# Queries as rows of eight tokens, weights in 512 KB pieces, output rows in threes, mp by head pairs

## The chip, the cores and the metric

The kernel runs on one core of a Trainium2 chip. The metric is the device time of one execution in microseconds. Its parts are named by their engines: PE is TensorE (PEld its weight loads), DVE is VectorE, ACT is ScalarE, POOL is GpSimd, SP is SyncE, whose queue issues all DMAs of this kernel.

## What is computed

Attention through 32 packed queries per head, and then a soft mixture of experts over all tokens, all in float32:

```
batch, n_heads, seq, head_dim = 8, 8, 576, 64;  n_pack = 32      # q, k, v: [8, 8, 576, 64], p: [8, 8, 32, 64]
N, D, E, S_per_e, F = 4608, 512, 8, 4, 1024                      # phi: [512, 32], w1: [8, 512, 1024], w2: [8, 1024, 512]

p_packed = sm_attn(p, k, v)                 # softmax(p k^T / 8) v
out      = sm_attn(q, p_packed, p_packed)   # softmax(q p_packed^T / 8) p_packed
x = out.transpose(0, 2, 1, 3).reshape(4608, 512)

logits = x @ phi                            # [4608, 32]
d = softmax of logits over the tokens;  slot_input = d.T @ x
h = relu(slot_input[e] @ w1[e]);  slot_out[e] = h @ w2[e]        # 4 slots for each of 8 experts
c = softmax of logits over the slots
return c @ slot_out                         # [4608, 512]
```

## The kernel before

The batches go in four pairs (`dd`) and the heads in two groups of four (`g`), so that there are eight steps `i = 2 dd + g`, each with both batches of its pair (`b2`). A step loads k, q and v tiles (lines 105 to 142), each in a main tile of 1 MB from a pool `ring` of 15 buffers and a small tail tile of 128 KB; the tails of v and q share six buffers (`NTAIL`). All loads are issued by SP in program order. A main tile of v and of q holds for each of 128 partitions four tokens of a head side by side (runs of 1 KB); the tail holds the last 64 tokens of a head in 64 partitions per batch.

For each step, `kp` transposes k, `s1` makes the first scores and their exponentials, `ap` and `at` transpose those, `ppm` multiplies with v, `ppn` and `pt` (lines 302 to 328) normalise the packed rows and transpose them into `ppT`, in which the two halves of the partitions (the first token's 64 columns and the second's) stand in two separate slots `x`, the rest being zero. `mp` (line 330) multiplies `ppT` with `phi`, head by head. `qp` (line 348) transposes q in 18 blocks of 128 columns, two tokens in each, and `s2p` (line 367) multiplies them with `ppT` in three chunks `c` (two with four rows of tokens, one with the ninth). `a2p` and `lg` give the logits, and the functions `f1` to `gsa` carry the softmax over the tokens from one pair to the next. The steps are interleaved by hand in the loop from line 752 on: the loads of step i + 1 stand at its head, the loop works step i, and the last step and what follows stand in an order written out by hand.

The weights come in 32 chunks of 1 MB (`load_w`, line 720), each in four DMAs of 256 KB with runs of 2 KB. They go to `ring` buffers as these come free, and to buffers of pools that close. The first three are issued in the last turn of the loop, between the main tiles and the tails of v and q of step 7 (lines 761 to 765). Layer 1 (`layer1a`, line 977) and layer 2 (`layer2`, line 1032) take the chunks in order; the last expert's second layer (`last2`, line 1116) is split in column halves and ends the work on weights.

After the softmax over the slots, `cq` and `cp` (lines 1050 to 1072) split and transpose its result into `cT`, nine blocks of 128 tokens for each pair, and `slot_out` (line 1147) multiplies each block with the slots' rows into a 256 KB tile of the output. Eight of the nine blocks of a pair go out by batch, four rows per partition (runs of 8 KB, DMAs of 1 MB; the first four tiles singly, the first of them in two halves); the ninth blocks of all pairs are collected in `ot` and stored at the end by two DMAs of 512 KB, 64 partitions each, in runs of 2 KB. `evac` (line 81) shares the copies out of PSUM among ScalarE and VectorE.

Of the kernel before, what the change touches and what calls it, by code (L numbers as in the profile page):

```python
# [23 lines left out]
def pack_attention_soft_moe(  # L24
# [90 lines left out]
    def load_rows(src, i, name):  # L115

        dd, g = divmod(i, NG)
        main = ring.tile([P, 2, 4, TB * D], F32, tag="ring", name=f"{name}_{i}")
        for b2 in range(2):
            xs = src[2 * dd + b2, 4 * g : 4 * g + 4]  # L120
# [4 lines left out]
        return main  # L125

    def load_tail(src, i, name):
        dd, g = divmod(i, NG)
        tail = vpool.tile([P, 4, D], F32, tag="tail", bufs=NTAIL, name=f"{name}x_{i}")
        for b2 in range(2):  # L130
            xs = src[2 * dd + b2, 4 * g : 4 * g + 4]
# [4 lines left out]
        return tail  # L136

    def load_q(i):
        qts[i] = load_rows(q, i, "q"), load_tail(q, i, "q")

    def load_v(i):
        vts[i] = load_rows(v, i, "v"), load_tail(v, i, "v")
# [175 lines left out]
    def pt(i):  # L318

        s = st[i]  # L320
        tp = s["m"][:, P : 3 * P]
        for b2 in range(2):
            nc.tensor.transpose(
                tp[:, b2 * P : (b2 + 1) * P], s["ppd"][:, b2].rearrange("p x d -> p (x d)"), ident
            )
        tpv = tp.rearrange("p (b h s) -> p b h s", b=2, h=4)
        nc.vector.tensor_copy(ppT[0:D, :, :, 0, :], tpv[0:D])
        nc.vector.tensor_copy(ppT[D:P, :, :, 1, :], tpv[D:P])

    def mp(i):  # L330

        g = i % NG
        s = st[i]
        mq = s["m"][:, 3 * P : 3 * P + 2 * NSLOT]
        for b2 in range(2):
            for h in range(4):
                nc.tensor.matmul(
                    mq[32 * h : 32 * h + 32, b2 * NSLOT : (b2 + 1) * NSLOT],
                    ppT[:, b2, h, h % 2, :],
                    phi_sb[:, 2 * g + h // 2, :],  # L340
                    start=True,
                    stop=True,
                )
        mm = lpool.tile([P, 2, NSLOT], F32, tag="mm", bufs=2, name=f"mm_{i}")
        nc.scalar.copy(mm.rearrange("p b x -> p (b x)"), mq)
        s["mm"] = mm

    def qp(i, m0, eng=None):

        s = st[i]  # L350
        main, tail = qts[i]
        if m0 == 0:
            s["qT"] = tpool.tile([P, 2 * T, P], F32, tag="qT", name=f"qT_{i}")
        qf = (main if m0 < 16 else tail).rearrange(
            "p b h x -> p (b h x)" if m0 < 16 else "p h x -> p (h x)"
        )
# [10 lines left out]
    def s2p(i, c):  # L367
# [384 lines left out]
    for i in range(NSTEP - 1):  # L752
# [297 lines left out]
    def cq(t0, nt=4):  # L1050
# [10 lines left out]
        for x in range(0, nt, 4):  # L1061
            c4s[t0 + x] = c4[:, x : x + 4]

    def cp(t0, eng="act"):
        tp = bank(pstr, f"cp_{t0}")
        for j in range(4):
            nc.tensor.transpose(
                tp[:, j * P : (j + 1) * P].bitcast(F32R),
                c4s[t0][:, j].rearrange("p a b s -> p (a b s)"),
                identr,  # L1070
            )
        evac(cT[:, t0 : t0 + 4].rearrange("p t x -> p (t x)"), tp, eng)

    with tc.manual_schedule(engines={EP.PE, EP.DVE, EP.Activation, EP.Pool}):
# [14 lines left out]
        for t0 in (0, 4):  # L1089
            cp(t0)  # L1090
# [54 lines left out]
    ot = ring.tile([P, ND, DM], F32, tag="ring", name="ot")  # L1145
# [6 lines left out]
    todo = list(range(8, NT, 4))  # L1152
    for dd in range(ND):
        for b2 in range(2):
            ob = ring.tile([P, TB, DM], F32, tag="ring", name=f"ob_{dd}_{b2}")
            r0 = (2 * dd + b2) * S
            ov = out[r0 : r0 + TB * P].rearrange("(p t) m -> p t m", t=TB)
            for t in range(TB):
                o = 4 * (t % 2) + 2 * b2 + t // 2
                if (dd, b2, t) == (0, 0, 0):  # L1160

                    for xs, eng in zip(halves, ("act", "dve")):
                        op = bank(pstr, f"op_0_0_0_{eng}")
                        nc.tensor.matmul(op[:, xs], cT[:, o, :], sh[:, xs], start=True, stop=True)
                        evac(ob[:, t, xs], op[:, xs], eng)
                        nc.sync.dma_start(out=ov[:, t, xs], in_=ob[:, t, xs])
                    continue
                slot_out(ob[:, t], f"{dd}_{b2}_{t}", dd * T + o)
                n = 1 if (dd, b2) == (0, 0) else TB
                if (t + 1) % n == 0:  # L1170
                    ts = slice(t + 1 - n, t + 1)
                    nc.sync.dma_start(out=ov[:, ts], in_=ob[:, ts])
            for x in range(2 if dd == 0 else 1):
                if todo:
                    cp(todo.pop(0), None)
        slot_out(ot[:, dd], f"{dd}", dd * T + T - 1)
    for b2 in range(2):
        nc.sync.dma_start(
            out=out.rearrange("(a b s) m -> b s a m", b=2, s=S)[b2, TB * P : S],
            in_=ot[b2 * R : (b2 + 1) * R],  # L1180
        )
# [32 lines left out]
```

## Time and profile before

| what | value |
|---|---|
| median of three runs | 227.0 us (225.78, 227.0, 228.66) |
| the profiled execution, whole time | 227.74 us |
| its span, first to last instruction | 225.9 us |
| its mean granted TensorE clock | 0.953 |
| busy, share of the span | PE 85%, DVE 53%, ACT 51%, POOL 11% |
| moved by DMA | 72.36 MB, mean 320 GB/s |

A share of busy time is a mean over stages that have different limits, so it is read together with the slices, the chain of waits and the single stretches. Times inside the profile count from the start of the span. The terms of the working below are in the profiled execution's own time, which is 0.7 us above the median.

### The profile page before, as it was taken

The page shows a single profiled execution, that of the slowest core. Times are in us where ns is not written, and L with a number is a line of the kernel's source. Part 1 is how long each engine was busy: PE and PEld are TensorE (multiplying, and loading weights), DVE is VectorE, ACT ScalarE, POOL GpSimd, SP SyncE. Part 2 cuts the span into 40 slices and gives each one's busy share as a digit, 9 for nine tenths or more (in the row PEclk, how much of TensorE's full clock was granted, in tenths as well). Part 3 has the DMA queues.
Part 4 walks back from the last instruction along what each step waited for, and adds up shares of the span by engine and source line. Part 5 has one row for each costly group of instructions (what it writes and reads, how often), then busy time and mean ns, then how long its engine had stood idle before and what let it go on. Part 6 is the DMA issues. An engine that isn't in the chain of part 4 may idle for free.

```text
span 225.9 us, 6900 instructions
## 1 busy us (share of the span) xinstructions
PE 191.9 (85%) x2875; PEld 129.6 (57%) x2875; DVE 120.3 (53%) x279; ACT 115.9 (51%) x253; POOL 25.1 (11%) x40
## 2 busy tenths in 40 slices
PE   1897799898996999999999989988899999899500
PEld 1665577585683678668678758766534333465200
DVE  2220576257287146728956626896777260388500
ACT  2377536956843475684675694755322100288500
POOL 3000003103003000300210120042030000000000
PEclk9999979999998599999999999999999999999955
DMA  4999999999999999999799999999999999089996
GB/s 134 299 273 311 323 304 315 282 285 317 284 320 272 335 291 331 314 366 326 218 328 382 377 389 380 364 369 357 384 354 376 385 392 375 25 281 418 424 395 159
DMA packets 52624, 72.36 MB, mean 320 GB/s; under 512 B 12656, under 2 KB 32368, under 8 KB 51696
## 3 DMA queue, kind: packets, MB, share of 16 engines
q1 hardware_dynamic: 52592, 71.91, 98.6%
q8 instruction: 23, 0.38, 0.7%
q14 instruction: 9, 0.07, 0.1%
HBM read 62.46 MB, written 9.44 MB: 318 GB/s over the span
## 4 chain that ended last, share of the span: by engine, by line
PE 63%; ACT 16%; DVE 6%; DMA 4%; issue 3%; SPq 1%; ACTq 0%; DVEq 0%
PE s L380 9%; PE kp L220 8%; PE s L240 7%; PE hp L987 6%; PE so L1036 5%; ACT a L251 5%; PE m L294 4%; PE op L1149 3%; PE qp L361 3%; PE gr L634 3%; ACT kT L88 3%; DMA k<-in_k_dram 2%; ACT qT L88 2%; PE a2p L452 2%; PE ap L269 2%
## 5 line engine op out<-in xcount | busy, mean ns | idle before, releaser
L88 ACT COPY kT<-kp 128x512 f32<-128x512 f32 (+1 forms) x42 | 19.1, 483 | 25.3 <-PE kp L220 25.3
L443 POOL TENSOR_TENSOR a<-a,z 128x1152 f32<-128x1152 f32 (+1 forms) x8 | 16.0, 1995 | 72.5 <-DVE z L442 50.1
L380 PE MATMUL s<-ppT,qT 128*64 128x64 f32 x576 | 21.3, 231 | 1.4 <-ACT qT L88 0.9
L220 PE MATMUL kp<-ident,k 128*128 128x128 f32 x128 | 20.9, 307 | 1.9 <-DMA k<-in_k_dram 0.9
L88 ACT COPY qT<-qp 128x512 f32<-128x512 f32 (+1 forms) x40 | 20.3, 559 | 4.1 <-PE qp L361 3.8
L380 PEld LDWEIGHTS s<-ppT,qT 128*64 128x64 f32 x576 | 19.1, 144 | 4.9 <-ACT qT L88 3.5
L251 ACT ACTIVATE a<-s,nm 128x576 f32<-128x576 f32 x16 | 21.6, 1350 | 0.5 <-DVE nm L247 0.5
L247 DVE TENSOR_REDUCE nm<-s 128x1 f32<-128x576 f32 x16 | 11.9, 746 | 18.0 <-PE s L240 18.0
L240 PE MATMUL s<-kT,pT 64*32 64x288 f32 x256 | 17.4, 446 | 3.8 <-ACT kT L88 3.2
L220 PEld LDWEIGHTS kp<-ident,k 128*128 128x128 f32 x128 | 16.1, 157 | 7.3 <-issue 2.3
L390 DVE TENSOR_REDUCE mx<-s 128x16 f32<-128x512 f32 (+1 forms) x24 | 12.6, 551 | 12.5 <-PE s L380 12.4
L361 PE MATMUL qp<-ident,q 128*128 128x128 f32 x128 | 18.4, 281 | 0.0
L88 ACT COPY a1T<-ap 128x512 f32<-128x512 f32 x16 | 8.7, 588 | 18.8 <-PE ap L269 18.8
L361 PEld LDWEIGHTS qp<-ident,q 128*128 128x128 f32 x128 | 15.4, 146 | 1.9 <-issue 1.9
L987 PE MATMUL hp<-w,xz 128*32 128x512 f32 x128 | 14.8, 594 | 0.5 <-DVE xz L1075 0.5
L435 DVE TENSOR_REDUCE z<-a 128x36 f32<-128x1152 f32 (+2 forms) x9 | 10.9, 1207 | 6.2 <-ACT a L426 6.2
L1036 PE MATMUL so<-w,hT 128*32 128x512 f32 x112 | 12.4, 592 | 0.0
L1149 PE MATMUL op<-sh,cT 128*128 128x512 f32 x35 | 11.9, 444 | 0.2 <-ACT ob L88 0.2
L452 PE MATMUL a2p<-ident,a 128*128 128x128 f32 x72 | 11.0, 280 | 0.6 <-ACT a L412 0.6
L88 ACT COPY ob<-op 128x512 f32<-128x512 f32 x19 | 10.7, 588 | 1.6 <-PE op L1149 0.5
L88 ACT COPY a2T<-a2p 128x512 f32<-128x512 f32 (+1 forms) x24 | 11.1, 514 | 0.6 <-PE a2p L452 0.5
L396 DVE TENSOR_TENSOR a<-s,mx 128x512 f32<-128x512 f32 (+1 forms) x21 | 10.9, 549 | 0.1
(155 smaller groups left out, 302.0 us busy)
## 6 DMA issues: line engine op xcount, KB each, us to landing
w<-in_moe_w_dram SPq DMA_DIRECT2D x128, 256.0 KB, 5.4
k<-in_k_dram SPq DMA_DIRECT2D x16, 512.0 KB, 6.6
q<-in_q_dram SPq DMA_DIRECT2D x16, 512.0 KB, 7.3
v<-in_v_dram SPq DMA_DIRECT2D x16, 512.0 KB, 8.1
out_dram<-ob SPq DMA_DIRECT2D x7, 1024.0 KB, 6.6
kx<-in_k_dram SPq DMA_DIRECT2D x16, 64.0 KB, 6.3
qx<-in_q_dram SPq DMA_DIRECT2D x16, 64.0 KB, 7.1
vx<-in_v_dram SPq DMA_DIRECT2D x16, 64.0 KB, 6.7
```

The costliest lines, as they stand in the source:

```text
L88: nc.scalar.copy(dst, src)
L220: nc.tensor.transpose(tp[:, j * P : (j + 1) * P], src, ident)
L240: nc.tensor.matmul(ps[hs, x, 0:HALF], pTs[dd][xs, g, 4 * b2 + h].rearrange("p a s -> p (a s)"), kT[xs, :, hs], start=True, stop=True,)
L251: nc.scalar.activation(a1.rearrange("p (r t x) -> p x t r", t=T, x=2), ps[:, :, 0:HALF].rearrange("p x (t r) -> p x t r", t=T), AF.Exp, bi ...
L361: nc.tensor.transpose(tp[:, j * P : (j + 1) * P], qf[:, o : o + P], ident)
L380: nc.tensor.matmul(ps[us, j * 64 : j * 64 + 64], s["qT"][:, 8 * c + j, us], w, start=True, stop=True)
L390: nc.vector.tensor_reduce(mx, s[f"s2{c}"], axis=AX.X, op=ALU.max)
L443: eng.tensor_tensor(a2, a2, z2.unsqueeze(3).broadcast_to([P, nt, 4, NS]), op=ALU.mult)
L452: nc.tensor.transpose(tp[:, j * P : (j + 1) * P], s["a2"][:, t0 + j].rearrange("p h s -> p (h s)"), ident)
L987: nc.tensor.matmul(hp[nh][32 * a : 32 * a + 32, :], xzf[:, (4 * e + a) * NSLOT : (4 * e + a + 1) * NSLOT], w1s[e, a // 2][:, a % 2, nh * 5 ...
L1036: nc.tensor.matmul(so[32 * a : 32 * a + 32, :], hTf[:, (NJ * e + j) * NSLOT : (NJ * e + j + 1) * NSLOT], w2s[e, j // 4][:, j % 4, :], star ...
L1149: nc.tensor.matmul(op, cT[:, o, :], sh, start=True, stop=True)
```

## The change

The query tiles are loaded as rows of eight tokens: a partition holds nine tokens that follow each other in one head, eight in the main tile (runs of 2 KB) and the ninth in the tail; two heads fill the 128 partitions. `s2p` takes the transposed blocks accordingly, and the two slots of `ppT` are exchanged, so that two heads' slots lie side by side and `mp` takes two heads in one product. The weights are loaded in pieces of 512 KB with runs of 4 KB. In the last turn of the loop the tails of v and q stand with their main tiles, ahead of the first three weights. The output has nine tokens in each partition of a pair, and goes out in pieces of three rows over 128 partitions (768 KB, runs of 6 KB; the first three rows singly); `ot` is gone, and the transposes `cp` are regrouped to match, with `cpt` for the ninth blocks.

```diff
-    def load_rows(src, i, name):
+    def load_q(i):
         dd, g = divmod(i, NG)
-        main = ring.tile([P, 2, 4, TB * D], F32, tag="ring", name=f"{name}_{i}")
+        main = ring.tile([P, 2, 2, 8 * D], F32, tag="ring", name=f"q_{i}")
+        tail = vpool.tile([P, 2, 2, D], F32, tag="tail", bufs=NTAIL, name=f"qx_{i}")
+        for t, o, n in ((main, 0, 8 * D), (tail, 8 * D, D)):
+            for b2 in range(2):
+                xs = q[2 * dd + b2, 4 * g : 4 * g + 4].rearrange(
+                    "(a x) (r t) d -> (x r) a (t d)", a=2, t=T
+                )
+                nc.sync.dma_start(out=t[:, b2], in_=xs[:, :, o : o + n])
+        qts[i] = main, tail
...
-        nc.vector.tensor_copy(ppT[0:D, :, :, 0, :], tpv[0:D])
-        nc.vector.tensor_copy(ppT[D:P, :, :, 1, :], tpv[D:P])
+        nc.vector.tensor_copy(ppT[0:D, :, :, 1, :], tpv[0:D])
+        nc.vector.tensor_copy(ppT[D:P, :, :, 0, :], tpv[D:P])
...
         for b2 in range(2):
-            for h in range(4):
+            for a in range(2):
                 nc.tensor.matmul(
-                    mq[32 * h : 32 * h + 32, b2 * NSLOT : (b2 + 1) * NSLOT],
-                    ppT[:, b2, h, h % 2, :],
-                    phi_sb[:, 2 * g + h // 2, :],
+                    mq[64 * a : 64 * a + 64, b2 * NSLOT : (b2 + 1) * NSLOT],
+                    ppT[:, b2].rearrange("p h x s -> p (h x s)")[:, (4 * a + 1) * NS : (4 * a + 3) * NS],
+                    phi_sb[:, 2 * g + a, :],
...
                 if c < 2:
-                    w = ppT[:, c, j // 2]
+                    m, x = 8 * c + 4 * (j // 4) + 2 * u + j % 2, j // 2 % 2
+                    w = ppT[:, c, j // 2, ::-1]
+                    o = ps[us, j * 64 : j * 64 + 64]
                 else:
-                    w = ppT[:, u].rearrange("p h x s -> p (h x) s")[:, 4 * j : 4 * j + 4 : 3]
+                    m, x = 16 + u, j
+                    w = ppT[:, u].rearrange("p h x s -> p (h x) s")[:, 2 * x + 1 : 2 * x + 5 : 3]
+                    o = ps[us, 0:P].rearrange("p (a x s) -> p x a s", a=2, x=2)[:, x]
                 nc.tensor.matmul(
-                    ps[us, j * 64 : j * 64 + 64], s["qT"][:, 8 * c + j, us], w, start=True, stop=True
+                    o, s["qT"][:, m, 64 * x : 64 * x + 64], w, start=True, stop=True
                 )
...
-                for x in range(2):
-                    xs = slice(x * FF // 2, (x + 1) * FF // 2)
-                    nc.sync.dma_start(out=t[:, y, xs], in_=w1[e, r0 : r0 + P, xs])
+                nc.sync.dma_start(out=t[:, y], in_=w1[e, r0 : r0 + P])
...
-            for j in range(NJ // 2):
-                nc.sync.dma_start(out=t[:, j], in_=wv[:, c * (NJ // 2) + j])
+            for j in range(0, NJ // 2, 2):
+                j0 = c * (NJ // 2) + j
+                nc.sync.dma_start(out=t[:, j : j + 2], in_=wv[:, j0 : j0 + 2])
...
         else:
-            mains = load_rows(v, i + 1, "v"), load_rows(q, i + 1, "q")
+            load_v(i + 1)
+            load_q(i + 1)
             for x in order[:NAHEAD]:
                 load_w(ring, *x)
-            vts[i + 1] = mains[0], load_tail(v, i + 1, "v")
-            qts[i + 1] = mains[1], load_tail(q, i + 1, "q")
...
+    def cp(dd, u, eng="act"):
+        tp = bank(pstr, f"cp_{dd}_{u}").bitcast(F32R)
+        tv = tp.rearrange("p (j w b r) -> p j b w r", j=2, w=2, b=2)
+        for j in range(2):
+            for b2 in range(2):
+                nc.tensor.transpose(tv[:, j, b2], c4s[T * dd + 4 * j + 2 * b2 + u], identr)
+        evac(
+            cTv[:, dd, 0:8].rearrange("p (w t) x -> p t w x", w=2)[:, 2 * u : 2 * u + 2],
+            tp.bitcast(F32).rearrange("p (j w x) -> p j w x", j=2, w=2),
+            eng,
+        )
...
-    ot = ring.tile([P, ND, DM], F32, tag="ring", name="ot")
...
+    todo = [(cpt, ())] + [(cp, (dd, u)) for dd in range(1, ND) for u in range(2)]
     for dd in range(ND):
+        ov = out[2 * S * dd : 2 * S * (dd + 1)].rearrange("(p t) m -> p t m", t=T)
+        for t in range(T):
+            j = t % 3
+            if j == 0:
+                ob = ring.tile([P, 3, DM], F32, tag="ring", name=f"ob_{dd}_{t}")
...
+            slot_out(ob[:, j], f"{dd}_{t}", T * dd + t)
+            if (dd, t // 3) == (0, 0):
+                nc.sync.dma_start(out=ov[:, t], in_=ob[:, j])
+            elif j == 2:
+                nc.sync.dma_start(out=ov[:, t - 2 : t + 1], in_=ob)
+            if j == 2 and todo:
+                f, x = todo.pop(0)
+                f(*x, None)
```

## Rows read from the trace of the kernel before

**Rows 1.** The page: busy time by engine; busy tenths of DMA in 40 slices.

```profile
PE 191.9 (85%) x2875; PEld 129.6 (57%) x2875; DVE 120.3 (53%) x279; ACT 115.9 (51%) x253; POOL 25.1 (11%) x40
DMA  4999999999999999999799999999999999089996
```

**Rows 2.** The page: chain of work that ended last, by engine.

```profile
PE 63%; ACT 16%; DVE 6%; DMA 4%; issue 3%; SPq 1%; ACTq 0%; DVEq 0%
```

**Rows 3.** Waits of TensorE for loads: us in total, times, longest us.

```profile
PEld so L1036 <- DMA w<-in_moe_w_dram: 1.4, 5, 0.3
PE kp L220 <- DMA k<-in_k_dram: 0.9, 1, 0.9
```

**Rows 4.** Timeline of TensorE, 190 to 200 us: start us, us, engine, line.

```profile
193.70 1.07 PE L1117 MATMUL sb<-w,hT 128*32 128x256 f32 x16
```

**Rows 5.** Windows: engines' busy us (instructions); last PEclk, DMA share, GB/s.

```profile
104.00:116.00 12.00, 11.75 (x211) 8.34 (x211) 9.49 (x26) 8.63 (x20) 2.37 (x2) 1.00 0.89 264
166.00:192.00 26.00, 26.00 (x252) 10.04 (x248) 11.91 (x30) 3.41 (x5) 2.24 (x2) 1.00 1.04 380
192.00:194.00 2.00, 2.00 (x24) 1.03 (x18) 0.59 (x1) 0.00 (x0) 0.00 (x0) 1.00 0.19 70
203.00:219.00 16.00, 8.72 (x35) 4.56 (x34) 8.42 (x13) 8.25 (x15) 0.00 (x0) 0.87 1.01 420
219.00:225.00 6.00, 0.00 (x0) 0.00 (x0) 0.00 (x0) 0.00 (x0) 0.00 (x0) 0.50 0.76 214
...
224.00:225.00 1.00, 0.00 (x0) 0.00 (x0) 0.00 (x0) 0.00 (x0) 0.00 (x0) 0.50 0.09 33
```

**Rows 6.** Timeline of SP's queue, 196 to 226 us.

```profile
197.77 0.83 SPq L1166 DMA_DIRECT2D out_dram<-ob  x2
...
212.89 2.72 SPq L1178 DMA_DIRECT2D out_dram<-ot  x2
```

**Rows 7.** DMA issues: count, KB each, median us from issue to landing.

```profile
out_dram<-ot SPq DMA_DIRECT2D x2, 512.0 KB, 10.4
```

**Rows 8.** Groups by line and shape: busy us, mean ns; idle before, releaser.

```profile
L380 PE MATMUL s<-ppT,qT 128*64 128x64 f32 x576 | 21.3, 231 | 1.4 <-ACT qT L88 0.9 <-DVE ppT L328 0.3
L240 PE MATMUL s<-kT,pT 64*32 64x288 f32 x256 | 17.4, 446 | 3.8 <-ACT kT L88 3.2 <-ACT a L251 0.5
L361 PEld LDWEIGHTS qp<-ident,q 128*128 128x128 f32 x128 | 15.4, 146 | 1.9 <-issue 1.9
L269 PEld LDWEIGHTS ap<-ident,a 128*128 128x128 f32 x64 | 8.4, 208 | 1.1 <-ACT a L251 0.8
L337 PE MATMUL m<-phi_sb,ppT 128*32 128x32 f32 x128 | 2.9, 201 | 1.0 <-DVE ppT L328 1.0
L685 PE MATMUL gr<-rb,ppd 128*64 128x64 f32 x48 | 2.2, 230 | 0.0
```

**Rows 9.** Timeline of SP's queue, 86 to 108 and 56 to 196 us.

```profile
92.60 11.18 SPq L729 DMA_DIRECT2D w<-in_moe_w_dram  x12
104.17 1.26 SPq L132 DMA_DIRECT2D vx<-in_v_dram  x2
...
106.83 25.83 SPq L729 DMA_DIRECT2D w<-in_moe_w_dram  x36
```

**Rows 10.** Timeline of all engines, 88 to 108 us: q's tail of step 4.

```profile
98.14 0.38 PE L361 MATMUL qp<-ident,qx 128*128 128x128 f32 x2
```

**Rows 11.** Waits of SP's queue: us in total, times, longest us.

```profile
SPq L735 <- PE hp L987: 2.0, 1, 2.0
SPq L735 <- PE qp L361: 1.8, 3, 0.7
```

**Rows 12.** Window as in rows 5, in the middle of the attention.

```profile
72.00:78.00 6.00, 5.91 (x55) 3.49 (x55) 1.32 (x4) 2.42 (x5) 0.24 (x2) 0.50 1.05 328
```

**Rows 13.** Timeline of all engines, 62 to 82 us: before that window.

```profile
69.88 2.13 POOL L443 TENSOR_TENSOR a<-a,z 128x1152 f32<-128x1152 f32 x1 [9.62 <-ACT a1tail L283]
...
70.15 1.89 DVE L579 TENSOR_SCALAR rw<-rep,w,zg 128x32 f32<-128x32 f32 x1 [0.42 <-ACT w L570]
```

More of the change, by code (lines that the diff above doesn't have):

```diff
@@ L113, in load_k, with load_v @@
         kts[i] = (main, tail)
-    def load_rows(src, i, name):
+    def load_q(i):
         dd, g = divmod(i, NG)
-        main = ring.tile([P, 2, 4, TB * D], F32, tag="ring", name=f"{name}_{i}")
+        main = ring.tile([P, 2, 2, 8 * D], F32, tag="ring", name=f"q_{i}")
[7 more added lines that the diff above has]
+        qts[i] = main, tail
+    def load_v(i):
+        dd, g = divmod(i, NG)
+        main = ring.tile([P, 2, 4, TB * D], F32, tag="ring", name=f"v_{i}")
+        tail = vpool.tile([P, 4, D], F32, tag="tail", bufs=NTAIL, name=f"vx_{i}")
         for b2 in range(2):
-            xs = src[2 * dd + b2, 4 * g : 4 * g + 4]
+            xs = v[2 * dd + b2, 4 * g : 4 * g + 4]
             nc.sync.dma_start(
@@ L124, in load_rows @@
             )
[L125 to L129, printed above, removed]
         for b2 in range(2):
-            xs = src[2 * dd + b2, 4 * g : 4 * g + 4]
+            xs = v[2 * dd + b2, 4 * g : 4 * g + 4]
             nc.sync.dma_start(
@@ L135, in load_tail @@
             )
[L136 to L142, printed above, removed]
+        vts[i] = main, tail
     load_p(0)
@@ L353, in qp @@
             s["qT"] = tpool.tile([P, 2 * T, P], F32, tag="qT", name=f"qT_{i}")
-        qf = (main if m0 < 16 else tail).rearrange(
-            "p b h x -> p (b h x)" if m0 < 16 else "p h x -> p (h x)"
-        )
+        qf = (main if m0 < 16 else tail).rearrange("p b a x -> p (b a x)")
         nt = min(4, 2 * T - m0)
@@ L1060, in cq, with cpt @@
         nc.vector.tensor_copy(c4[:, :, 1], c4f[:, :, 0])
[L1061 to L1066, printed above, removed]
+        for x in range(nt):
+            c4s[t0 + x] = c4[:, x].rearrange("p a b s -> p (a b s)")
+    cTv = cT.rearrange("p (a t) x -> p a t x", a=ND)
+    def cp(dd, u, eng="act"):
[9 more added lines that the diff above has]
+        )
+    def cpt(eng="act"):
+        tp = bank(pstr, "cp_t")
+        for dd in range(ND):
             nc.tensor.transpose(
-                tp[:, j * P : (j + 1) * P].bitcast(F32R),
-                c4s[t0][:, j].rearrange("p a b s -> p (a b s)"),
-                identr,
+                tp[:, dd * P : (dd + 1) * P].bitcast(F32R), c4s[T * dd + T - 1], identr
             )
-        evac(cT[:, t0 : t0 + 4].rearrange("p t x -> p (t x)"), tp, eng)
+        evac(cTv[:, :, T - 1], tp.rearrange("p (a x) -> p a x", a=ND), eng)
     with tc.manual_schedule(engines={EP.PE, EP.DVE, EP.Activation, EP.Pool}):
@@ L1088, in pack_attention_soft_moe @@
         layer1a(QE, [QE])
-        for t0 in (0, 4):
-            cp(t0)
+        for u in range(2):
+            cp(0, u)
         layer1a(QE, [QE + 1])
@@ L1150, in slot_out @@
         evac(dst, op)
-    todo = list(range(8, NT, 4))
+    todo = [(cpt, ())] + [(cp, (dd, u)) for dd in range(1, ND) for u in range(2)]
     for dd in range(ND):
[L1154 to L1181, printed above, removed]
+        ov = out[2 * S * dd : 2 * S * (dd + 1)].rearrange("(p t) m -> p t m", t=T)
[3 more added lines that the diff above has]
+                ob = ring.tile([P, 3, DM], F32, tag="ring", name=f"ob_{dd}_{t}")
+            if (dd, t) == (0, 0):
+                for xs, eng in zip(halves, ("act", "dve")):
+                    op = bank(pstr, f"op_0_0_{eng}")
+                    nc.tensor.matmul(op[:, xs], cT[:, 0, :], sh[:, xs], start=True, stop=True)
+                    evac(ob[:, j, xs], op[:, xs], eng)
+                    nc.sync.dma_start(out=ov[:, t, xs], in_=ob[:, j, xs])
+                continue
+            slot_out(ob[:, j], f"{dd}_{t}", T * dd + t)
[6 more added lines that the diff above has]
+                f(*x, None)
```

## The prediction, made before the change was run

> **What bounds the kernel now.** I read the page's busy time and slices first. TensorE is busy 85% of the span, and the DMA engines are full in nearly every slice up to the 34th of 40, empty for one, and full again to the end [rows 1]. Two resources look like a bound at once, so the next view is the chain of work that ended last: 63% of it lies on TensorE, 16% on ScalarE, 4% on DMA [rows 2]. Then the waits say who waited for a load. In all of the load phase TensorE waited 0.9 us for one k tile at the start, and the largest other group is five waits of 0.3 us (1.4 us in all) in layer 2 [rows 3]; there the same short gap of 0.28 us stands between all groups of four weight loads, whatever is named, so I don't count it as a wait for data. Up to the last layer, then, full DMA queues hide behind TensorE. How narrowly, the windows tell: the loads run at 380 GB/s up to 192 us and die out between 192 and 194 [rows 5], and the second half of the last expert's matmuls, which uses the last weights, starts at 193.70 [rows 4]. The load stream is about 1 us ahead.
>
> At the end it is the other way round. The last issue of an output piece starts at 212.89, when all output tiles are computed [rows 6], but the DMA engines store until 224 [rows 5]. The store runs at 420 GB/s from 203 to 219 and at 214 GB/s from 219 to 225 [rows 5]. That last stretch is the two pieces of `ot`, 512 KB each, 10.4 us from issue to landing [rows 7]: 64 partitions each, 2 KB runs. So the span is a TensorE chain to the first store at 197.77 us [rows 6], then a store that is limited by the DMA engines.
>
> **The change part by part.**
>
> *Output rows in threes.* `ot` goes; the ninth row goes out with its neighbours, in pieces of 768 KB over 128 partitions with 6 KB runs. The stretch from 219 to 225 moved 6 x 214 = 1.28 MB, and ended near 224.1 (share 0.09 in the last window) [rows 5]: 5.1 us. At the 420 GB/s of the stretch before it, 1.28 MB takes 3.06 us. That is 2.0 us off the end. What could eat it: the 6 KB run stands in no row. Its bounds are the 8 KB runs (420 GB/s) and the 2 KB runs of the weights (380 GB/s) [rows 5]. The 11 pieces of 768 KB are 8.65 MB: 20.6 us at 420, 22.8 us at 380, so 0 to 2.2 us lost. I take 0.1 us, since 6 KB is nearest to the 8 KB row. One single-row piece fewer at the start gives about as much back. The producers don't set the pace: 36 tiles and 7 copies of cT are done in 198 to 212.9 [rows 6], 0.35 us each, so a group of three with its transposes is ready every 1.4 us, and its store takes 786 KB / 420 = 1.9 us. The reordered `cp` transposes and copies are as many and as wide as before: nothing. Sum here: 2.0 us less.
>
> Which of the two differences makes the `ot` stretch slow, its 2 KB runs or its 64 partitions, the row alone doesn't say; either is gone in the changed kernel, so the sum stands without an answer. The Trainium skill, "SBUF — State Buffer", section "Door 1: The DMA port swizzle", says that a range of 64 partitions reaches only 8 of 16 ports and gives about 218 GB/s where 128 partitions have 436. The 214 GB/s agrees with that [rows 5]. By the page's figures (an estimate) 1.28 MB would go from 5.9 us to 2.9 us, so 3 us instead of 2.
>
> *mp by head pairs.* Before, 128 matmul instructions in the run, 2.9 us busy, 22.6 ns each [rows 8]. After, 64 with stationary operands twice as wide. Such an operand stands in two rows: 2.2 us / 48 = 46 ns each (line 685) and 21.3 / 576 = 37 ns (line 380) [rows 8]. Bounds: 64 x 46 = 2.9 us, nothing saved; 64 x 22.6 = 1.4 us, 1.5 us saved. I take 37 ns, the row with the most instances: 2.4 us, 0.5 us saved; with 63% of the chain on TensorE [rows 2], 0.3 us. Each product now needs both `ppT` copies instead of one; the matmuls of qp and s1 stand between the copies and mp, and where less does, the first product waited for line 328, the later of the two copies, already before (1.0 us in the run) [rows 8].
>
> *s2p.* As many matmuls, of the same shapes. The moving operand now takes its two runs of 32 floats in falling order (`::-1`), and the ninth row's output is written in runs of 32. No row has a falling step. Below: nothing, since line 240 reads its moving operand in runs of 32 floats too and takes 17.4 us / 256 = 68 ns for 288 columns, less per column than line 380 (37 ns for 64) [rows 8]. Above: a stepped operand that costs is that of line 269, 208 ns against 146 ns of line 361 for the same weight load [rows 8], 1.42 times; on the 512 of 576 instructions touched, 21.3 x 512/576 x 0.42 = 8 us. I take 0: line 269 steps every float, this one keeps runs.
>
> *Query loads and weight pieces.* q's runs go from 1 KB to 2 KB, the weights' from 2 KB to 4 KB, and 64 of 128 weight DMAs on SP go. For the weights, 33.6 MB at 380 GB/s are 88 us; the bounds of the new rate are the same 380 and the 420 of 8 KB runs [rows 5], 0 to 8 us of DMA time. In the span I count 0 for both, because TensorE waits for no load; the cover is the chain of matmuls to 193.70. If this cover were gone, the loads would end the phase and 0 to 8 us would count.
>
> *Order in the last load step.* Before, three weights stood ahead of the tails of v and q of step 7. Now the tails stand first, and SP issues in order. The tails have six buffers; q's tail of step 7 takes that of step 4, whose last readers run from 98.14 to 98.5 [rows 10]. So the first weight, issued at 92.60 before [rows 9], comes at 98.5 plus 1.3 us for two tail DMAs, 99.8: 7.2 us later. Behind it stand all weights, and for them wait both layers of the experts. But the 2.7 us of tails at 104.17 to 106.83 are then past [rows 9], and three weights take 11.2 us as before: the fourth comes at 111.0 instead of 106.83, 4.2 us later. What absorbs it: before, the stream itself stood for ring buffers from 104 to 116 (264 instead of 380 GB/s, 3.7 us) [rows 5], later 1.8 and 2.0 us for qp and layer 1 [rows 11], and it was 1 us ahead at the end: 8.5 us in all. I take 0.
>
> **Sum**, against the profiled execution's own span of 225.9 us: 225.9 - 2.0 - 0.3 = 223.6 us. That execution took 227.74 us in all, 1.8 us around its span and 0.7 us above the median of 227.0. On the median: 224.7 us.
>
> **The rivals.**
>
> *The clock doesn't fall.* The granted clock was 0.50 from 72 to 78 us (1.2 instead of 2.4 GHz), TensorE busy all through it [rows 12]; before that it stood while DVE's rw took 1.89 us [rows 13] beside a POOL instruction that began 0.27 us earlier. Were rw first, half of 6 us and up to 1.5 of rw's 1.89 us would go: 224.7 less 3 to 4.5, about 221. For it: mp shortens the steps a little, and 0.27 us is little. Against: DVE's queue holds the reduction that POOL waits for ahead of rw, and the change doesn't touch that. Chance 0.15.
>
> *Smaller pieces eat the gain.* 15 output DMAs instead of 14, 6 KB runs at the lower bound: the 2.2 us come back, 226.9, no change. The pieces overlap in the queue at 420 GB/s, which speaks against it. Chance 0.10. The Trainium skill, SBUF page, "The DMA setup-cost knee", gives each transfer some 2 us of its own; one more DMA, unhidden, would make the sum 226.7. The trace shows no such gaps between queued pieces: seven of 1 MB keep 420 GB/s [rows 5].
>
> *The weights come late* (slower). Place: SP behind q's last tail. Price: each us beyond the 8.5 us of cover counts whole. It decides when the hold-up is over 8.5 us instead of 4.2, or when the ring gives buffers back too late to catch up; with nothing absorbed 224.7 + 4.2 = 228.9, with 7.2 us 231.9. Chance 0.12, most of it within 2%.
>
> *The falling operand costs* (slower). Place: line 380. At the upper bound 224.7 + 8 = 232.7; over 2% slower from 6.8 us, that is 13 ns for each of 512 instructions. Chance 0.08.
>
> **How the numbers follow.** Forecast 0.55, at 224.7 us; its own range, from the output's bounds and mp's, is 223.5 to 226.5. Rivals 0.15, 0.10, 0.12, 0.08. The range 221.2 to 227.8 holds the forecast, the second rival, most of the first and about half of the third; the operand and the worst of the weights are left out. About 2% is what a measurement of this kernel can tell from no change (222.5 and 231.5). Faster by more: 0.17, the clock rival and a margin. Slower by more: 0.10, the operand and the tail of the weights. Within: 0.73.
>
> **What would show it.** Output: no stretch of the store near 214 GB/s, and the end 11 to 12 us after the last output issue instead of 13. mp: half the instructions at 35 to 40 ns each. s2p: line 380 stays near 21.3 us; above 23 us the operand costs. Order: SP stands before the q tail until about 98.5, and no new wait of layer 1 or 2 for w; a wait there of more than 1 us makes the prediction wrong to the slow side. If TensorE's chain reaches the first output matmul much before 196 us, loads or the clock had a price that I put at nothing.

## The result, and the profile after

The changed kernel took 223.48 us (median of 20 runs, 221.68 to 226.88), the kernel before beside it 228.48 us (20 runs, two of which took 570 us, and no run says why). The ratio is 0.9853 [0.9818, 0.9887]: faster by 1.5%, or 3.4 us, and by the medians 5.0 us. A second comparison (the runs of `a0_after` below) gave 222.93 against 228.34 us and 0.976 [0.971, 0.981], 5.4 us by the medians. The forecast was 224.7 us, 2.3 us less than before: the time lies inside its range, but more was gained than its sum has. Ratios leave out the runs over 1.5% above the fastest of the same kernel, which leaves 8 of the 20 runs of before in the first comparison, its shortest, and all 11 in the second, so that the first ratio shows less than the medians do; the profiles marked * below are of such longer executions, and from those only rates and waits are read, no end.

The profiled execution of the changed kernel took 222.83 us, its span is 221.1 us (before 225.9), and its granted clock 0.970 (before 0.953). The page, busy time, DMA slices and chain by engine, beside [rows 1, 2]:

```profile
PE 188.4 (85%) x2811; PEld 127.8 (58%) x2811; DVE 120.5 (54%) x279; ACT 116.3 (53%) x253; POOL 25.0 (11%) x40
DMA  4999999999999999579999989999789999159996
PE 53%; ACT 17%; DVE 10%; DMA 7%; issue 4%; SPq 3%; ACTq 0%; DVEq 0%
```

SP's queue (start us, us, what it issued), beside [rows 6, 9]:

```profile
95.44 0.88 SPq L125 DMA_DIRECT2D qx<-in_q_dram  x2
96.37 31.07 SPq L734 DMA_DIRECT2D w<-in_moe_w_dram  x24
...
194.75 0.83 SPq L1181 DMA_DIRECT2D out_dram<-ob  x2
```

Windows of the changed kernel, columns as in [rows 5]; last PEclk, DMA share, GB/s:

```profile
28.00:34.00 6.00, 5.75 (x127) 4.80 (x128) 4.08 (x11) 4.24 (x7) 0.24 (x1) 1.00 1.11 323
72.00:80.00 8.00, 8.00 (x101) 5.85 (x100) 2.80 (x6) 5.24 (x10) 0.24 (x1) 0.84 1.10 342
90.00:96.00 6.00, 5.40 (x67) 4.37 (x61) 2.81 (x6) 5.03 (x10) 2.37 (x2) 1.00 0.67 201
104.00:116.00 12.00, 12.00 (x177) 8.64 (x175) 8.96 (x24) 8.70 (x22) 2.61 (x3) 1.00 1.03 410
116.00:130.00 14.00, 12.99 (x253) 10.07 (x252) 8.26 (x16) 9.35 (x22) 2.37 (x2) 1.00 0.99 387
190.00:195.00 5.00, 3.93 (x28) 2.19 (x27) 1.49 (x4) 1.49 (x4) 0.00 (x0) 1.00 0.02 4
203.00:219.00 16.00, 5.86 (x21) 2.93 (x20) 5.94 (x9) 5.89 (x11) 0.00 (x0) 0.75 1.01 413
219.00:225.00 6.00, 0.00 (x0) 0.00 (x0) 0.00 (x0) 0.00 (x0) 0.00 (x0) 0.66 0.01 3
```

The first two of these windows in the first profile of the kernel before:

```profile
28.00:34.00 6.00, 5.75 (x76) 4.78 (x73) 3.97 (x10) 2.56 (x5) 0.24 (x1) 0.78 1.12 305
72.00:80.00 8.00, 7.91 (x81) 4.95 (x89) 2.16 (x6) 3.43 (x8) 0.24 (x2) 0.60 1.07 320
```

And the groups by line that answer to [rows 8]:

```profile
L387 PE MATMUL s<-ppT,qT 128*64 128x64 f32 x576 | 20.6, 225 | 1.1 <-DVE ppT L331 0.3
L340 PE MATMUL m<-phi_sb,ppT 128*64 128x32 f32 x64 | 3.4, 228 | 1.0 <-DVE ppT L331 1.0
```

The 4.8 us between the two spans lie in two places. The first store is 3.0 us earlier (194.75 against 197.77), and from there to the end it takes 26.3 us instead of 28.1, 1.8 us less. The second is the output term. The first isn't in the sum. In this pair of profiles it has a plain cause: before, the clock was 0.78 from 28 to 34 us and 0.60 from 72 to 80 us, after it was 1.00 and 0.84. As an estimate, a mean of 0.78 is 2.6 of 6 us at the lower level (1.2 of 2.4 GHz), where half of the work is lost, so 1.3 us; 0.60 and 0.84 make 3.2 and 1.3 us. The number of products from 72 to 80 us agrees roughly: 81 at 0.60, 101 at 0.84, and 118 to 146 in the profiles with 1.00, as in `a0_after`, the second one of the changed kernel:

```profile
72.00:80.00 8.00, 8.00 (x125) 6.16 (x119) 3.33 (x9) 6.07 (x13) 0.47 (x2) 1.00 1.09 337
```

The difference is 3.2 us, which would explain all of it. Whether the change made the clock better, or one execution of each happened to differ, a pair can't tell. The experiments went there.

### The profile page after: what moved, and what is told of

The parts are those of the page before. It is cut to its first block, busy times and chain, and to the rows that moved or that the text cites. A ratio compares the mean times of both kernels' runs of the same rounds, so it can differ in the third digit from the quotient of the medians.

```text
span 221.1 us, 6708 instructions
## 1 busy us (share of the span) xinstructions
PE 188.4 (85%) x2811; PEld 127.8 (58%) x2811; DVE 120.5 (54%) x279; ACT 116.3 (53%) x253; POOL 25.0 (11%) x40
## 4 chain that ended last, share of the span: by engine, by line
PE 53%; ACT 17%; DVE 10%; DMA 7%; issue 4%; SPq 3%; ACTq 0%; DVEq 0%
PE s L387 8%; PE kp L223 6%; PE s L243 6%; DMA v<-in_v_dram 6%; PE so L1040 5%; ACT a L254 5%; PE m L297 3%; PE op L1165 3%; ACT kT L88 3%; PE gr L641 3%; PE hp L991 2%; ACT qT L88 2%; PE ap L272 2%; PE lp L479 2%; ACT a1T L88 2%
## 5 line engine op out<-in xcount | busy, mean ns | idle before, releaser
L387 PE MATMUL s<-ppT,qT 128*64 128x64 f32 x576 | 20.6, 225 | 1.1 <-DVE ppT L331 0.3
L387 PEld LDWEIGHTS s<-ppT,qT 128*64 128x64 f32 x576 | 18.3, 138 | 4.8 <-ACT qT L88 3.7
L243 PE MATMUL s<-kT,pT 64*32 64x288 f32 x256 | 16.8, 437 | 3.8 <-ACT kT L88 3.0
L442 DVE TENSOR_REDUCE z<-a 128x36 f32<-128x1152 f32 (+2 forms) x9 | 10.9, 1207 | 6.4 <-ACT a L433 6.4
L1165 PE MATMUL op<-sh,cT 128*128 128x512 f32 x35 | 12.7, 455 | 0.8 <-DVE cT L91 0.3
L91 DVE COPY ob<-op 128x512 f32<-128x512 f32 x17 | 11.3, 689 | 1.3 <-PE op L1165 0.9
L297 PE MATMUL m<-v,a1T 128*32 128x64 f32 x512 | 9.7, 221 | 1.9 <-ACT a1T L88 1.4
```

The lines of the kernel that those rows point to most:

```text
L243: nc.tensor.matmul(ps[hs, x, 0:HALF], pTs[dd][xs, g, 4 * b2 + h].rearrange("p a s -> p (a s)"), kT[xs, :, hs], start=True, stop=True,)
L297: nc.tensor.matmul(s["m"][hs, b2 * D : (b2 + 1) * D], s["a1T"][:, 4 * b2 + j, hs] if j < 4 else a1tail[:, b2, hs], vm[:, b2, h, j * D : (j ...
L387: nc.tensor.matmul(o, s["qT"][:, m, 64 * x : 64 * x + 64], w, start=True, stop=True)
L1165: nc.tensor.matmul(op, cT[:, o, :], sh, start=True, stop=True)
```

## Experiments

**The output: 64 partitions, or short runs?** The changed kernel again (`a0_after`), then with the end of the output as before, eight rows in pieces of four and the ninth rows collected in `ot` and stored by two DMAs of 64 partitions (`a1_ot64`), then with `ot` stored by one DMA over 128 partitions, still in runs of 2 KB (`a2_ot128`):

```diff
+    ot = ring.tile([P, ND, DM], F32, tag="ring", name="ot")
...
+        slot_out(ot[:, dd], f"{dd}", T * dd + T - 1)
+    o9 = out.rearrange("(a p t) m -> p a t m", a=ND, t=T)[:, :, T - 1]
+    for b2 in range(2):                                  # a1_ot64
+        rs = slice(b2 * R, (b2 + 1) * R)
+        nc.sync.dma_start(out=o9[rs], in_=ot[rs])
...
+    nc.sync.dma_start(out=o9, in_=ot)                    # a2_ot128
```

> The changed kernel again, as the yardstick for the runs beside it. In its first profile the first output store began 3.0 us earlier than before (194.75 against 197.77) and the time from there to the end was 26.3 us instead of 28.1. The theory of the output end and the clock together: about 222 to 225 us, the spans of single runs differing with the granted clock (a run with 0.98 some 1.5 us under one with 0.97). The theory that faster loads brought the 3 us: the same time, but the 3 us stay whatever the granted clock of a run is.

> The changed kernel with the end of the output as before: eight rows of a partition in two 1 MB pieces of four rows, and the ninth rows of all pairs collected and stored at the end by two DMAs of 64 partitions with runs of 2 KB. Theory of the prediction (the output end is worth 2.0 us): 2.0 us slower than the changed kernel, all of it after the last output tile, with a stretch near 214 GB/s at the end. Rival (smaller pieces and 6 KB runs cost as much as they bring): no difference. Nothing before the first store changes by either.

> As the kernel with the two 64-partition DMAs, but the ninth rows leave by one DMA over 128 partitions, still in runs of 2 KB. If the 64 partitions make the slow stretch: back to within 0.5 us of the changed kernel (1.05 MB at some 380 instead of 420 GB/s is 0.3 us more). If the runs of 2 KB make it: as slow as with 64 partitions, 2.0 us over the changed kernel.

Measured: 222.93, 225.07 and 223.28 us; ratios 0.976 [0.971, 0.981], 0.9856 [0.9806, 0.9907], 0.9763 [0.9718, 0.9809]. So the 64-partition end costs 2.1 us by the medians (2.2 by the ratios) and the 128-partition `ot` next to nothing. Windows at the end, first of `a1_ot64`, then of `a2_ot128`*:

```profile
203.00:214.00 11.00, 4.70 (x15) 2.04 (x14) 4.75 (x7) 4.49 (x9) 0.00 (x0) 0.93 1.01 416
...
216.00:217.00 1.00, 0.00 (x0) 0.00 (x0) 0.00 (x0) 0.00 (x0) 0.00 (x0) 0.50 0.92 199
217.00:218.00 1.00, 0.00 (x0) 0.00 (x0) 0.00 (x0) 0.00 (x0) 0.00 (x0) 0.50 0.90 191
218.00:219.00 1.00, 0.00 (x0) 0.00 (x0) 0.00 (x0) 0.00 (x0) 0.00 (x0) 0.50 0.98 295
```

```profile
209.00:219.00 10.00, 5.21 (x19) 2.54 (x18) 5.26 (x8) 5.00 (x10) 0.00 (x0) 0.97 1.00 414
219.00:224.00 5.00, 0.00 (x0) 0.00 (x0) 0.00 (x0) 0.00 (x0) 0.00 (x0) 0.50 1.01 403
...
222.00:223.00 1.00, 0.00 (x0) 0.00 (x0) 0.00 (x0) 0.00 (x0) 0.00 (x0) 0.50 1.02 383
223.00:224.00 1.00, 0.00 (x0) 0.00 (x0) 0.00 (x0) 0.00 (x0) 0.00 (x0) 0.50 1.04 391
```

With 64 partitions the rate falls from 416 to 191 to 199 GB/s, and to 295 for one microsecond between, while the DMA engines are 90% busy or more. The 214 GB/s of [rows 5] is a mean over such a stretch. With 128 partitions the 1 MB of `ot`, in the same runs of 2 KB, is the end of the store, and goes at 383 to 391 GB/s (403 is a mean with rows of 8 KB before it). So it is the partitions; the runs of 2 KB cost little. The Trainium skill, "SBUF — State Buffer", section "Door 1: The DMA port swizzle", on which the prediction draws, gives 64 partitions half the ports of 128. The runs agree, with about half the rate.

**mp by pairs.** Taken out of the changed kernel (`a3_mp1`), and alone in the kernel before, with the exchanged slots and the falling operand (`b6_mp2`):

```diff
-            for a in range(2):
-                nc.tensor.matmul(
-                    mq[64 * a : 64 * a + 64, b2 * NSLOT : (b2 + 1) * NSLOT],
...
+            for h in range(4):                           # a3_mp1
+                nc.tensor.matmul(
+                    mq[32 * h : 32 * h + 32, b2 * NSLOT : (b2 + 1) * NSLOT],
+                    ppT[:, b2, h, 1 - h % 2, :],
+                    phi_sb[:, 2 * g + h // 2, :],
```

> The changed kernel with mp head by head again (8 products of 32 columns in a step instead of 4 of 64). Prediction's term: 0.3 us slower, 128 instructions of 23 ns busy each instead of 64 of 37. If the order of the first step, which the pairs change too, decided whether the granted clock falls early: the stretch at 1.2 GHz near 28 us comes back and it is 1.7 us slower.

> The kernel before with the edit of mp alone: two heads in one product, the slots of ppT exchanged, and s2p's moving operand with its two runs in falling order. Theory that it is worth next to nothing: ratio 0.997 to 1.000, s2p's line at 20.5 to 21.5 us busy, mp's at 3 to 3.5 us with half the instructions. Rival that it is worth its 0.3 to 0.5 us and more by the clock: 0.990 or less. Rival that the falling operand costs behind the loads' cover: over 1.004.

Measured: `a3_mp1` 223.5 us, 0.9776 [0.973, 0.9823], 0.4 us (by the ratios) behind the changed kernel; `b6_mp2` 227.43 us, 0.9974 [0.994, 1.0009]. Both point to some half microsecond gained, and both intervals reach to nothing. In the profile of `a3_mp1` the clock is 1.00 from 28 to 34 us as in the changed kernel, and in a second profile of the kernel before (`c0_before`, below) too, so it isn't mp that keeps the clock there. In `b6_mp2` mp's products are busy for 3.9 us, more than the 3 to 3.5 expected:

```profile
L337 PE MATMUL m<-phi_sb,ppT 128*64 128x32 f32 x64 | 3.9, 228 | 1.2 <-DVE ppT L328 1.0
```

**The loads.** Before again (`c0_before`); before with nothing but the weights' pieces of the changed kernel (`b5_w4k`); the changed kernel with the old piece and run lengths of the weights and runs of 1 KB for q (`a5_loads`; q's pieces are 256 KB there, which they weren't before), and with those of the weights alone (`a6_w2k`):

```diff
-                for x in range(2):
-                    xs = slice(x * FF // 2, (x + 1) * FF // 2)
-                    nc.sync.dma_start(out=t[:, y, xs], in_=w1[e, r0 : r0 + P, xs])
+                nc.sync.dma_start(out=t[:, y], in_=w1[e, r0 : r0 + P])       # b5_w4k
...
-            for j in range(NJ // 2):
-                nc.sync.dma_start(out=t[:, j], in_=wv[:, c * (NJ // 2) + j])
+            for j in range(0, NJ // 2, 2):
+                j0 = c * (NJ // 2) + j
+                nc.sync.dma_start(out=t[:, j : j + 2], in_=wv[:, j0 : j0 + 2])
```

> The kernel before, profiled once more. In the timed runs so far its time was 227.3 to 230.2 us with granted clocks of 0.954 to 0.976, the longest with the highest, while the changed kernel needs 222 to 223.7 at 0.971 to 0.976. Theory of the clock (the 3 us on TensorE's side are its phases at 1.2 GHz): the output stores begin near 197.8 again, with one or two stretches at 1.2 GHz before 100 us, and near 194.5 if there are none. Theory of the loads (the stream of weights, 1 us ahead of the matmuls in the first profile, sets the end of layer 2 in most runs): with a high clock the first store is no earlier, TensorE waits for w in layer 1 or 2 by 1 to 4 us, and the loads die out later than 193.

> The kernel before with one edit: weights in pieces of 512 KB with runs of 4 KB. The prediction put this at 0 us, since TensorE waited for no load. Theory of the loads: 2 to 4 us faster than before, the weights at 400 to 415 GB/s instead of 380, and the loads over some 4 us earlier. Theory of the clock: no difference beyond 0.5 us.

> The changed kernel with short runs in the loads: q's main tiles in runs of 1 KB (each DMA halved), weights in 256 KB pieces with runs of 2 KB, everything else as changed, the tails ahead of the first weights too. Theory of the loads: 2 to 4 us slower than the changed kernel (225 to 227 us), with waits of layer 1 or 2 for w; more if the tails ahead of the weights then cost as well. Theory of the prediction and of the clock: within 0.5 us of the changed kernel (about 223).

> The changed kernel with the weights alone back in 256 KB pieces with runs of 2 KB; q keeps its 2 KB runs. Theory that the weights' run length sets when layer 1 gets its weights: ratio to the kernel before 0.983 to 0.986 (the changed kernel itself 0.976 on one chip and 0.985 on another, where with q's runs undone too it was 0.984), 1.5 to 2 us slower than the changed kernel; waits of TensorE's line hp for w return, 2 us or more in all; weights at 350 to 385 GB/s. Rival that q's runs made the difference: ratio as the changed kernel, 0.976, no such waits. Rival that neither counts and TensorE's clock made it: ratio as the changed kernel wherever the granted clock is as high.

Measured: 228.85 us, 0.9996 [0.9954, 1.0039]; `b5_w4k` 227.8 us, 0.9882 [0.9813, 0.9951]; `a5_loads` 224.65 us, 0.9836 [0.9794, 0.9879]; `a6_w2k` 224.09 us, 0.9788 [0.973, 0.9845]. The weights' edit alone makes the kernel before 2.7 us faster by the ratio (0.8 by the medians). That size is rough: the ratio counts three of six runs, and the six had a granted clock of 0.955 on the mean, while the runs of before beside them had 0.967. Undone, it costs the changed kernel 0.6 to 1.2 us, and with q's 1.2 to 1.7, against its two medians and the ratio of `a0_after`; since the changed kernel's ratio was 0.976 in one comparison and 0.9853 in the other, these two sizes aren't firm, and q's share isn't told apart. Both are below what was expected of them (1.5 to 2 us and 2 to 4), and `a6_w2k` has no wait at hp again, only 2.0 us at sb and 0.6 at so. What the profiles show is firmer. Waits of TensorE's weight loads for `w` (us in total, times, longest) in `c0_before`*:

```profile
PEld hp L987 <- DMA w<-in_moe_w_dram: 5.1, 6, 1.3
PEld so L1036 <- DMA w<-in_moe_w_dram: 1.1, 4, 0.3
```

in `b6_mp2` and in `b4_rwact` (below), at hp:

```profile
PEld hp L987 <- DMA w<-in_moe_w_dram: 4.8, 6, 1.3
```

```profile
PEld hp L986 <- DMA w<-in_moe_w_dram: 5.4, 7, 1.4
```

in `a5_loads`:

```profile
PEld hp L994 <- DMA w<-in_moe_w_dram: 2.8, 5, 1.4
PEld so L1043 <- DMA w<-in_moe_w_dram: 0.8, 3, 0.3
```

and in the changed kernel, first profile:

```profile
PEld hp L991 <- DMA w<-in_moe_w_dram: 0.3, 1, 0.3
PEld so L1040 <- DMA w<-in_moe_w_dram: 0.3, 1, 0.3
```

So the kernel before does wait for its weights in layer 1, in a second execution of the very same code, and the one on which the prediction was made [rows 3] is the exception among the four profiles of before with weights in 2 KB runs. All the profiles together, by the weights' runs (waits of PEld for `w` at hp, so and sb; the share of `w` in the chain of work that ended last, where `w` is among the lines shown there):

| profile | weights' runs | clock | waits for w, us | w in the chain | first store, us |
|---|---|---|---|---|---|
| before, first | 2 KB | 0.953 | 1.7 | - | 197.77 |
| before again* | 2 KB | 0.959 | 6.2 | 26% | |
| before, mp alone | 2 KB | 0.970 | 5.6 | 25% | 199.24 |
| before, rw on ScalarE | 2 KB | 0.975 | 6.5 | 41% | 197.04 |
| changed, old loads | 2 KB | 0.975 | 3.6 | 30% | 197.26 |
| changed, old weights* | 2 KB | 0.955 | 2.6 | 10% | |
| before, new weights* | 4 KB | 0.949 | 0.3 | - | |
| changed, first | 4 KB | 0.970 | 0.6 | - | 194.75 |
| changed again | 4 KB | 0.976 | 0.8 | - | 194.08 |
| changed, mp by heads | 4 KB | 0.974 | 0.6 | - | 194.00 |
| changed, `ot` of 64 partitions | 4 KB | 0.980 | 1.3 | - | 193.59 |
| changed, `ot` of 128 partitions* | 4 KB | 0.952 | 0.3 | - | |
| changed, old order | 4 KB | 0.974 | 1.0 | - | 195.41 |
| changed, rw on ScalarE | 4 KB | 0.978 | 1.4 | - | 193.63 |

The times of the runs say the same without a profile. In all 20 runs of the changed kernel the time falls as the mean granted clock rises, by 1.5 us for each 0.01, with a correlation of -0.81 (-1 would be a straight line, 0 no relation). In the 63 runs of the kernel before beside the experiments the correlation is -0.06: the 19 runs with a clock of 0.972 or more have a median of 228.86 us, the 21 under 0.965 one of 228.66. So TensorE's clock sets the time of the changed kernel, and something else sets that of the kernel before. With only the weights changed (`b5_w4k`) the relation is there, -0.99: its three runs under 0.955 take 228.5 to 229.86 us, no less than the nine such runs of before (median 228.64), but at 0.969 it takes 223.82, where before has 227.84 (median of 23 runs from 0.965 to 0.972). It stays with only the weights undone (`a6_w2k`, -0.95) and is gone with q's runs undone as well (`a5_loads`, 0.27). These are six runs each, too few to price q's share, but they don't say that it is nothing.

The rates of the weights while only they are loaded, windows of `c0_before`* and of `b5_w4k`*:

```profile
180.00:186.00 6.00, 6.00 (x67) 2.31 (x62) 2.24 (x5) 0.59 (x1) 0.00 (x0) 1.00 1.05 386
```

```profile
180.00:186.00 6.00, 6.00 (x68) 2.30 (x60) 3.85 (x10) 0.59 (x1) 0.00 (x0) 1.00 1.02 408
```

**TensorE earlier, in either kernel.** If loads and TensorE's chain are two limits side by side, then an earlier TensorE must gain in the changed kernel and nothing in the kernel before. The same edit in both, rw on ScalarE instead of VectorE beside GpSimd (`a4_rwact` in the changed kernel, `b4_rwact` in the kernel before):

```diff
-        nc.vector.tensor_scalar(
-            rw, rep[:, 0, :], x["w"], x["zg"], op0=ALU.mult, op1=ALU.mult
-        )
+        nc.scalar.mul(rw, rep[:, 0, :], x["w"])
+        nc.scalar.mul(rw, rw, x["zg"])
```

> The changed kernel with the product rw of f4 (1.9 us on VectorE beside a running POOL product, TensorE idle for 1.5 us behind it) made by two instructions on ScalarE. Theory of the clock: the wait of 1.5 us goes, and with it the stretch at 1.2 GHz behind it where there was one (3.4 us long in the changed kernel's first profile, half of which is lost): 1.5 to 3 us faster than the changed kernel, 220 to 221.5, with the granted clock at 1.00 from 66 to 80 us. If the stretch has another cause: only the 1.5 us or less.

> The kernel before with rw worked by two ScalarE instructions instead of one VectorE instruction beside GpSimd (the changed kernel gained 1.2 to 1.6 us by the same edit). Theory that the kernel before waits for its weights in layer 1: an earlier TensorE only waits longer there, so it gains 0 to 0.8 us, and TensorE's waits at hp and so for w grow to 3 us or more in its profile, although the granted clock has no stretch at 1.2 GHz near 70 us. Rival that TensorE's own chain and its clock set the end also in the kernel before: it gains 1.2 to 3 us.

Measured: changed 221.35 us, 0.9707 [0.9665, 0.9749], which is 1.2 us (ratio) to 1.6 us (median) less than without the edit, measured on another chip, and the interval of this difference reaches nothing; it was expected to be 1.5 to 3 us; before 228.99 us, 1.0051 [1.0008, 1.0093], no gain at all. The chain of work that ended last, by engine and by line, in `b4_rwact`:

```profile
DMA 62%; PE 17%; SPq 7%; ACT 5%; issue 2%; DVE 1%; ACTq 0%
DMA w<-in_moe_w_dram 41%; DMA k<-in_k_dram 8%; DMA q<-in_q_dram 7%; DMA v<-in_v_dram 4%; PE op L1148 3%; PE s L240 3%; SPq L121 2%; PE s L380 2%; SPq L728 2%; DMA out_dram<-ob 2%; PE kp L220 2%; SPq L132 1%; PE gr L633 1%; PE m L294 1%; PE sb L1116 1%
```

```profile
20.00:195.00 175.00, 163.85 (x2657) 108.81 (x2656) 96.98 (x238) 93.59 (x217) 22.41 (x25) 1.00 1.03 330
```

The granted clock is 1.00 here from 20 to 195 us, better than in the first profile of before (0.78 and 0.60 in places), and TensorE gets nothing for it but longer waits: 6.5 us for `w`. In the first profile of the kernel before, DMA had 4% of the chain [rows 2]. `a4_rwact`, with the same edit and weights in 4 KB runs, has 1.4 us of such waits and the shortest median of all these kernels. What the edit removes, rows of the timeline of the changed kernel (start us, us) and of `a4_rwact`:

```profile
68.24 2.13 POOL L450 TENSOR_TENSOR a<-a,z 128x1152 f32<-128x1152 f32 x1 [9.63 <-ACT a1tail L286]
68.51 1.89 DVE L586 TENSOR_SCALAR rw<-rep,w,zg 128x32 f32<-128x32 f32 x1 [0.42 <-ACT w L577]
```

```profile
67.95 0.32 ACT L586 ACTIVATE rw<-rep,w 128x32 f32<-128x32 f32 x1
68.30 0.32 ACT L587 ACTIVATE rw<-rw,zg 128x32 f32<-128x32 f32 x1
```

On VectorE, rw ends with the GpSimd instruction (70.40 and 70.37); on ScalarE it takes 0.32 us twice beside the same one. The Trainium skill, "SBUF — State Buffer", section "Who interferes with whom", says that VectorE and GpSimd share a pair of ports under an exclusive lock, and that ScalarE has its own; the rows agree.

TensorE waits 1.5 us for rw in the first profile of either kernel, and so the edit also takes away most of its idle time there. From 66 to 72 us it is busy for 4.28 us with rw on VectorE (first `a0_after`) and for 5.83 with rw on ScalarE (then `a4_rwact`):

```profile
66.00:72.00 6.00, 4.28 (x58) 2.59 (x56) 5.01 (x11) 2.91 (x10) 2.13 (x1) 1.00 1.08 319
```

```profile
66.00:72.00 6.00, 5.83 (x83) 3.33 (x86) 2.87 (x9) 3.90 (x10) 2.13 (x1) 1.00 1.10 292
```

Of the 12 profiles with rw on VectorE, nine show a granted clock under 1.00 between 66 and 80 us; neither of the two with rw on ScalarE does. Two are too few to show that this idle time brings the fall, but they don't rule it out.

**The order of the last load step.** The changed kernel with the tails of v and q behind the first three weights, as before (`a7_order`):

```diff
...
-            load_v(i + 1)
-            load_q(i + 1)
+            load_v(i + 1, 0)
+            load_q(i + 1, 0)
             for x in order[:NAHEAD]:
                 load_w(ring, *x)
+            load_v(i + 1, 1)
+            load_q(i + 1, 1)
```

> The changed kernel with the order of the last load step as before: the main tiles of v and q of step 7, then three weights, then the two tails. Theory that the hold-up behind the tails is absorbed: ratio as the changed kernel within 0.3%, no wait of TensorE for w in either; SP issues the first weight near 92 instead of 96 us, and the DMA engines move over 250 GB/s from 90 to 96 us instead of 201 to 210. Rival that the late weights cost: 1 to 4 us faster than the changed kernel. Rival that the order of before was worse, since the tails come late for the last step: 1 us or more slower, with a wait of TensorE for vx or qx.

Measured: 223.25 us, 0.9766 [0.972, 0.9812]: no difference from 222.93 us and 0.976. Windows of `a7_order`:

```profile
90.00:96.00 6.00, 5.39 (x68) 4.48 (x62) 2.62 (x6) 5.14 (x10) 2.37 (x2) 1.00 1.04 403
...
116.00:130.00 14.00, 12.99 (x253) 10.09 (x252) 8.15 (x16) 9.35 (x22) 2.37 (x2) 1.00 0.68 257
```

From 90 to 96 us it loads at 403 GB/s where the changed kernel stands at 201, from 96 to 104 at 342 against 286, and it pays that back from 116 to 130: 257 against 387 GB/s, while the stream stands for ring buffers. That is (403 - 201) x 6 + (342 - 286) x 8 = 1.7 MB early and (387 - 257) x 14 = 1.8 MB late: the stream gains nothing by starting early, since it then stands in front of full buffers.

## Why the prediction was right, and where it was not

The time lies inside the stated range, and just under the narrower one of 223.5 to 226.5 that came from the sum's own bounds. The gain of 3.4 to 5.5 us is larger than the 2.3 of the sum, so the range was met in part by its width.

*Output rows in threes, 2.0 us: right*, in size and mechanism. 1.8 us in the pair of profiles, 2.1 us undone. The end comes 10.9 us after the last output issue (210.2) instead of 13.0 after the first issue of `ot`. No stretch near 214 GB/s is left (413 from 203 to 219, then nothing), and the pieces of 768 KB keep the rate, so the rival that smaller pieces eat the gain falls. What the prediction left open is settled: 64 partitions, not 2 KB runs.

*mp by head pairs, 0.3 us: right within what can be measured, by a wrong duration.* The products take 3.4 us / 64 = 53 ns each, not 35 to 40, so mp's busy time rose from 2.9 to 3.4 us (3.9, or 61 ns each, in `b6_mp2`), and "half the instructions at 35 to 40 ns each" is wrong: the price is outside the bounds of 22.6 and 46 ns. What pays for that, so that neither run is slower with the pairs, no run shows. If the 0.3 us is there at all, it was met by luck.

*s2p's falling operand, nothing: right.* 20.6 us and 225 ns against 21.3 and 231 in the first profile of before, and 20.4 and 225 in `c0_before`. That rival falls.

*Order in the last load step, nothing: right*, and so is its reason, the absorption by buffers. The tails stood shorter than said: q's was issued at 95.44, not 98.5, since the last readers of step 4's tail ran from 95.03 to 95.41, and the first weight at 96.37. No wait of TensorE for w over 0.3 us came of it, and the rival of the late weights falls.

*Query loads and weight pieces, nothing: this is the step that failed.* Its reason was "because TensorE waits for no load", read from one execution [rows 3]. In that one TensorE was late, by the two stretches at the lower clock, and the load stream was 1 us ahead [rows 4, 5]. In three other profiles of before, or of before with an edit that doesn't touch the loads, TensorE waited 5.6 to 6.5 us for weights, and the chain ran over weight loads for 25% to 41%. The kernel before had two limits of about the same length: a TensorE chain whose clock differs from execution to execution, and a load stream at 380 GB/s. Whichever was longer set the first store, at 197 to 199 us, and over many runs a better clock brought it nothing. Runs of 4 KB raise the stream to 408 GB/s and take the second limit away, for the most part or wholly: 2.7 us in the kernel before (1.1 to 4.3 by its interval), inside the "0 to 8 us" that the prediction gave for the case that the cover is gone. With 2.1 us of the output and some 0.4 of mp that makes 5.2 us, beside 3.4 and 5.5 us by the two ratios. The prediction's own sign of this came: the first output matmul starts at 194.6 us, not 197.6, so "loads or the clock had a price that I put at nothing". Two things stay open: q's share, and what sets the end of the stream, which itself moves. The weights die out between 192 and 193 us in the first profile, between 193 and 194 in `b6_mp2`, and between 191 and 192 in `b4_rwact`.

*The clock rival: its condition came, its mechanism not.* In `a0_after` the clock is 1.00 from 20 to 195 us and the execution took 222.1 us, near the 221 that it gave; but rw still took 1.89 us beside GpSimd, so the clock can stay up without the rival's mechanism. Nor does the clock alone explain the gain: `b4_rwact` had it without any. Only with the weights in time does an earlier TensorE count: the runs' times beside their clocks show it, and `a4_rwact` points the same way. What makes the stretches come in some executions and not in others stays open.

## What to carry to other kernels

Where the profile shows one limit "1 us ahead" of another, don't price the edit that speeds up the hidden one at nothing: a second execution may have them the other way round, and every gain on the first is worth only as much as the second gives room for. Look at a second profile, or at whether the runs' times follow their clocks, before a load is called hidden. Here the stores wanted 128 partitions, and the weights' loads runs of 4 KB.

## What the runs showed of the hardware

- One core's weight loads ran at 366 to 388 GB/s in runs of 2 KB (pieces of 256 KB; six profiles, 180 to 186 us) and at 407 to 410 in runs of 4 KB (pieces of 512 KB; eight profiles), with the DMA engines full in both. Run and piece were not told apart.
- A store of 64 partitions went at 191 to 199 GB/s where it was slowest, one of 128 partitions in equal runs at 383 to 391.
- A float32 product with a stationary operand of 64 columns and a moving one of 32 took 53 to 61 ns of busy time, more than twice the 22.6 ns with 32 columns.
- A moving operand with two runs of 32 floats in falling order cost no more than a rising one (225 ns and 225 ns).
- The granted clock fell to its lower level in the same code in one execution and not in another (0.60 and 0.69 from 72 to 80 us in two of before, 0.84 and 1.00 in two of the changed kernel).
